# Nine pairs of token tiles instead of six in seven block products, with a new order for every queue

## The chip, the cores and the metric

The kernel runs on one core of one Trainium2 chip. A core has five engines, each with its own queue of instructions: TensorE (PE; weight loads are shown apart as PEld) does matmuls, VectorE (DVE) and ScalarE (ACT) do elementwise work, GpSimd (POOL) does the same more slowly, and SyncE (SP) issues DMAs. Engines wait for one another through semaphores. The metric is the device time of one execution in microseconds (us). Kernels are compared by the median of several executions.

## The reference

Two stages follow one another. The first is an attention with a window of 128 positions and 4 sink positions that every query sees; the second is a feed-forward layer with a swish-like gate over the 3072 tokens:

```python
scores = scale * np.matmul(q, k.transpose(0, 1, 3, 2))       # 4 batches, 8 heads, 768 positions, 64 wide
keep = is_sink | in_window                                   # 4 sinks, or 0 <= query - key < 128
a = softmax(np.where(keep, scores, -1e9))
attn = np.matmul(a, v)
x = attn.transpose(0, 2, 1, 3).reshape(3072, 512)
h = x @ w_in                                                 # 512 x 2048
g = h * (1.0 / (1.0 + np.exp(-beta * h)))
out = g @ w_out                                              # 2048 x 512
```

## The kernel before

The tokens are worked in eight half batches of 384 (T_ = 0 to 7). A half batch goes through these steps, each with one letter in the script:

- L, C: loads of q, k, v into staging buffers, and casts to bf16 (`load` L482, `cast`, whose copies stand at L405 for ACT, L407 for POOL, L410 for DVE). W: the same for the weights (`load_w` L494, `cast_w`).
- T or X: transposes of q and k, by PE for the first three half batches (L606, copied out by ACT or DVE), by DMA from SP after that (L589).
- S: scores of one or more tiles (L727, or L696 in a form by 64-row bands), the exponential on ACT (L739) into E, and the masks: L748 and L757 on DVE, or L754 on POOL.
- A: the products of E with v (L822) and of the sinks (L811, L795), then the division on DVE (L826, L828). R: the transpose of the result into xT, by PE (L847) or by DMA (L841).
- H: one of 16 slices of the first dense product, four matmuls of 384 columns (L864), a tanh on ACT (L870), and on DVE the product that makes g (L872).
- The second dense product. In the plain form, O, one tile of 128 tokens takes 16 matmuls of 512 columns (L884), in four steps of 4, then a copy out and a store (L893). In the pair form, P and Q, two tiles of 128 tokens are multiplied together as a 2 by 2 block product with seven block products instead of eight (`WP`): a block product is 8 matmuls of 256 columns (L965). The weights' sums T1, T2 and T4 stand in the buffers that staged the weights (L914), and T3 overwrites a quarter of the weights w_out16 (`last_w_sum`, L923, letter V), so V comes after the last plain product. For a pair, DVE makes four sums of g in place (L941), ACT or DVE three copies out of PSUM, and DVE five adds (four at L978, one at L1002). The block products of a pair stand in the order 4, 1, 2, 6, 7, 5, 3; a pair ends with its stores (L982).

Before the change the half batches 0 to 3 use the plain form and 4 to 7 the pair form: `FIRST = 4` gives six pairs, each of two tiles of one half batch, or of the third tiles of two neighbouring half batches (`PAIRS_OF`). Even pairs have the letter P, odd ones Q.

The order of work is written out by hand in strings. `SCRIPT` gives the order in which steps are recorded, and with it the numbers of the instructions and the rotation of buffers. `PE_ORDER` gives the order on PE; its letters s to z and digits are filler matmuls on constants (L1140), which compute nothing. `BANKS` gives the PSUM banks. `QUEUES` gives for ACT, DVE, POOL ("gp") and SP the instructions in their order, each as two digits in base 36. Some steps may stand on one of several engines, and the queue in which their number stands decides: a mask on DVE or POOL, a cast on ACT, DVE or POOL, a store on POOL or SP. `Graph.resolve` puts the semaphore waits in.

`Graph.emit` writes the queues. The last store on SP waits first until the earlier stores ("early") have landed; the program ends when the remaining ones ("late") have.

Of the kernel before, what the change touches and what calls it, by code (L numbers as in the profile page):

```python
# [34 lines left out]
class Graph:  # L35
# [241 lines left out]

SCRIPT = ("LLbLWLWLWLWLWLWLWLLWLLCCCCCCCCCBHTHHHTHTTHSHHHHSHHSHHHLWLWLWLLLLLAALWLAAHWOLWORLOLWRWULORROLCCCHHLHC"
          "CCHLHCOLHLCHHLCHHLTOLCTOCTOLCSCTLXXXXOCXOOCXSSCHHCAAHHCALARHLHOLROLORLRHLOOCXSOLCXOCXHCXSCXHCXHHHLHH"
          "LCHHLALRHRRHRHOCLCHHLCXHCXSOOLSLOOHLCXAAOCXHHRARROHCXOCXHOHOCOLOLOHHLLARHHLHHLLCHHLCHLHCXOLOCXSCXOOC"  # L280
          "XOCXOOCXSHLHCHLHHLHHLHHLHHLHHLHCHLHCOCXALCXOCXRRROROCXSCXOCXOOSOOCVAPRALHLHHHHAAHHRRCHPCPHHHHHPRHHHP"
          "PPSQQSHHHHHQQHHARHHHHRHRRHQHQHQHPPPPPPPHHHHHHHHHHQHHHQHHQHQQQQPPPPPPPQQQQQQQ")
# [4 lines left out]
BANKS = ("1740015236014523017646726136523054242315025450170467670132014560173462457371653706153776316745267452"  # L287
         "3002405057403613742674523014567230145023116757654030145231014574302711230656517245062245672303670145"
         "4502176436375401670514501672452375120145207370345213470456456701331016723015264327051670523511676245"
         "45023176523417605304271640135403")  # L290
QUEUES = {"act": ("010w0305070z16101119121b1e1h1i1k1n1w1q1t32303133272a3c3l3p3q2h3v3u3y3a3e3g4c493m3i3s41434547384j4h4f"
                 "4p4m4w4t4y5q4r625h675b696c6h5l6k6p6t6v65716z8c6g6e5z8l8e748n787a7d7h7k8z8w7z818487887x7n8v9a96979tbf"
                 "9i9f9l9ecd9ya9ada4a1akahafamaratb6babdbkbmbrd7bvbyc1c6c9dec5d3etcfcqczcsd5d9dgdidpdrdudwe1e7e3eagjei"
                 "eheoelhhfbfefiflfnecfqfsfvfxf2f8f5g0g2g5g7gagde0gghziuh6h9hchsixhmhphli9i6ibifidilinisizj1hjj3j5j7jb"
                 "jdjfjxk0kllslvjojrjujnk2k8k5kbkdkfkhkjkol1kql3l5l7lalilelmlqm6m8mamemgmcmkmimzmomtmmmqn5mvmxn1n3n7ng"
                 "njnunxnznl"),
          "dve": ("0x0y151813141f1x1d1y1c1z1l1p1m1o201s1r1u232124223525282629393d3k3o3r2b2c3x3b3f3h3z402q4a2s3j3n3t4244"
                 "462x4d3748364g4q4i5658575d595e5f5g5m614s505i684u5j5s6i6a5p6d5t6l5r6u6n6w646q5v728d5w70aq8f7c8o8m6s7j"
                 "7i7o8x907l8283867v7g858h898a8j8i8k5u8q8t8r8u9294989u9r9p9ha79g9n9va0aaaea59ca6a29m9kalaiagbh8bana3as"
                 "aub7bbbebl5xbnawbsayfhaxazb2b3b0b1bxbwc0bzapc2c8c7c3cackcbclcmcvcwcicndmdncocgcrd1ctdad0d6dhdjdqdsdv"  # L300
                 "dxe2e4e8ebf0ekejenemeqfceffffjfmfoftfrfwfyeyevhvg1g3g6g8gbgeghf9gngogtgpgqgrgugsi0i1ivhwh7j9jhjijjh4"
                 "h8iyhdhnhaiai7icigieimioitj0j2j4j6j8jcjejghxhyhoi3jyjzk1jlihiji4kmknlglhlkikiiltlolulwlxjsjplzjtjwly"
                 "m0k4k3k9jvkahukckekgkikkm1ksktkwkukpkvkxkykzkrl4l2l6m2l8m4lblfljm7lrlnm9mbmfmhmdmrmjmsmlmpn0mumnn6mw"
                 "myn2n4n8n9nanbncnhninenknvnwnynmnnnonpnqo0o2o3o4o6nso8"),
          "gp": ("0b0c0g0h0l0t0u0v0i0e0r0m0k0n0s0f0j0d0o0q0p171a1g1j1v342i2k2m2o4b2u4e3w4l4k4o4n666f6m7775796y8g7e7p7m"
                 "609z9jabbjbg7y8p9x9bbpbtced8erepe6faf3f7f6f4dbexglhqhthfgwgigyfghbgchehrjkjmjqiwk6irk7lllpm3m5ndnro5"
                 "nto9"),
          "sp": ("0002040608090a2d2e2f2g2j2l2n2p2r2t2v2w2y2z4v4x4z51525354555a5c5k5n7q6b5o635y766x6j6r6o7bdk807r7t7s7u"
                 "737w918y95938sao9s99aja87f9w9q9dacav9ob8ccbcb9b5biboc4b4cjd4cpbqe9cxbud2cudycydodtdlesdze5ddchegdceu"
                 "f1edewezgkdfg4h0h1h2h3fpgffufzg9fkeefdgmhih5hghkgzgxi2i8ipjaiqgvi5l0lcl9ldnfo1o7")}  # L310


def _program(nc, G, sb, ps, q, k, v, w_in, w_out, beta, out):
# [706 lines left out]
    def xl(hb):  # L1020
        if hb:
            if hb >= CUT:
# [158 lines left out]
```

## Time and profile before

| what | us |
|---|---|
| runs | 217.56, 219.13, 219.31 |
| median | 219.13 |
| the profiled execution | 218.22 |
| its span | 216.5 |
| PE busy in it | 207.1 |
| DVE busy | 166.9 |
| ACT busy | 145.5 |
| POOL busy | 53.8 |

The span runs from the first to the last instruction that the profile shows; the execution's own time is 1.7 us longer. Busy time of PE counts matmuls that are under way; since matmuls overlap one another, a busy PE is not always at its full rate. A group of the profile is a line of the kernel with its engine, operation and tiles; its row gives the count, the busy time, the mean duration in ns, and the engine's idle time just before, with what ended it.

### The profile page before, as it was taken

To read this page: it belongs to the slowest core of one execution; us is meant where nothing else is said; L and a number is where in the kernel's file an instruction comes from. 1 tells how busy PE (TensorE), PEld (TensorE's weight loads), DVE (VectorE), ACT (ScalarE), POOL (GpSimd) and SP (SyncE) were. 2 spreads that over 40 slices of the span, in tenths; PEclk is the share of its full clock that TensorE was granted. 3 is DMA by queue.
4 is the path that set the end of the run, shared out by engine and by line. 5 is a ranking of instruction groups with operands and counts; after the bars stand their busy time and mean duration, and the time that the engine had idled before them with its cause. 6 is when DMAs were issued, how large, how long until landed. Compare 5 with 4: busy or idle time off the path is not lost.

```text
span 216.5 us, 5121 instructions
## 1 busy us (share of the span) xinstructions
PE 207.1 (96%) x2022; PEld 131.2 (61%) x2040; DVE 166.9 (77%) x377; ACT 145.5 (67%) x252; POOL 53.8 (25%) x106
## 2 busy tenths in 40 slices
PE   8979999999999999999999999999999999999991
PEld 3546557555555455546654455865798666668881
DVE  1689899898794379966782587989898998788961
ACT  2899989959973696484585788488626957655210
POOL 7123653012610027100300117014802221000012
PEclk9999999999999999999999999999999999999999
DMA  6999999999989999947896797869985434100223
GB/s 189 257 326 368 353 268 345 380 289 214 215 200 124 221 208 210 188 102 158 151 200 129 148 225 182 173 143 254 193 177 117 98 118 113 40 3 0 97 76 121
DMA packets 94992, 39.90 MB, mean 184 GB/s; under 512 B 82088, under 2 KB 89528, under 8 KB 94968
## 3 DMA queue, kind: packets, MB, share of 16 engines
q1 hardware_dynamic: 92504, 34.33, 71.4%
q0 software_dynamic: 1376, 4.46, 6.4%
q10 hardware_dynamic: 1088, 0.79, 1.2%
q8 instruction: 16, 0.26, 0.5%
q14 instruction: 8, 0.07, 0.1%
HBM read 27.37 MB, written 6.29 MB: 156 GB/s over the span
## 4 chain that ended last, share of the span: by engine, by line
PE 74%; ACT 8%; DVE 8%; DMA 6%; issue 1%; SPq 1%; POOLq 0%; POOL 0%; ACTq 0%
PE P L864 31%; PE P L965 17%; PE P L884 13%; PE P L822 4%; DMA wst<-in_moe_w_out_dram 4%; PE P L696 3%; ACT E L739 3%; PE P L1140 3%; DVE g L872 2%; ACT qkT L405 2%; DMA xT<-onorm 2%; ACT t L870 1%; DVE E L757 1%; DVE E L748 1%; PE P L606 1%
## 5 line engine op out<-in xcount | busy, mean ns | idle before, releaser
L864 PE MATMUL P<-xT,w_in 128*128 128x384 bf16 x512 | 88.4, 326 | 0.9 <-DMA xT<-onorm 0.3
L870 ACT ACTIVATE t<-P,hbeta 128x384 f32<-128x384 f32 x128 | 67.5, 587 | 18.4 <-PE P L864 8.5
L872 DVE SCALAR_TENSOR_TENSOR g<-t,P 128x384 bf16<-128x384 f32 x128 | 64.8, 549 | 13.4 <-ACT t L870 12.6
L864 PEld LDWEIGHTS P<-xT,w_in 128*128 128x128 bf16 x512 | 48.4, 98 | 36.0 <-DMA xT<-onorm 1.4
L739 ACT ACTIVATE E<-P 128x1024 bf16<-128x1024 f32 x44 | 42.9, 1036 | 3.5 <-PE P L696 3.2
L884 PE MATMUL P<-w_out,g 128*128 128x512 bf16 x177 | 43.3, 379 | 1.0 <-issue 0.3
L405 ACT ACTIVATE osb<-P 128x256 f32<-128x256 f32 (+1 forms) x29 | 13.6, 476 | 33.0 <-PE P L965 19.3
L884 PEld LDWEIGHTS P<-w_out,g 128*128 128x128 bf16 x192 | 17.6, 98 | 18.8 <-issue 0.5
L757 DVE TENSOR_TENSOR E<-E,maskT 128x512 bf16<-128x512 bf16 x48 | 19.9, 447 | 8.3 <-ACT E L739 8.2
L754 POOL TENSOR_SCALAR_AFFINE_SELECT E<-E 128x512 bf16<-128x512 bf16 x24 | 16.0, 681 | 35.8 <-ACT E L739 35.8
L965 PE MATMUL P<-w_out,g 128*128 128x256 bf16 x192 | 24.3, 273 | 0.0
L965 PEld LDWEIGHTS P<-w_out,g 128*128 128x128 bf16 x192 | 18.5, 98 | 2.8 <-issue 0.2
L407 POOL TENSOR_SCALAR_AFFINE_SELECT q<-q_stage 128x512 bf16<-128x512 f32 x8 | 5.5, 693 | 56.1 <-DMA q_stage<-in_q_dram 56.1
L965 PE MATMUL P<-wst,g 128*128 128x256 bf16 x144 | 18.4, 273 | 0.0
L941 DVE TENSOR_TENSOR g<-g 128x1024 bf16<-128x1024 bf16 x24 | 16.3, 687 | 1.4 <-PE P L965 1.1
L828 DVE TENSOR_TENSOR onorm<-P,rden 128x384 bf16<-128x384 f32 x32 | 16.7, 546 | 0.3
L822 PEld LDWEIGHTS P<-vaug,E 128*128 128x128 bf16 x352 | 14.0, 97 | 2.8 <-DVE E L748 0.8
L982 POOL DMA_DIRECT2D out_dram<-osb x11 | 6.0, 543 | 37.8 <-DVE osb L978 32.3
L822 PE MATMUL P<-vaug,E 128*128 128x65 bf16 x352 | 15.1, 193 | 0.3 <-DVE E L748 0.3
L965 PEld LDWEIGHTS P<-wst,g 128*128 128x128 bf16 x144 | 13.8, 98 | 2.2
L978 DVE TENSOR_TENSOR osb<-P,osb 128x256 f32<-128x256 f32 x24 | 10.1, 422 | 4.4 <-PE P L965 4.2
L407 POOL TENSOR_SCALAR_AFFINE_SELECT vaug<-v_stage 128x512 bf16<-128x512 f32 x12 | 8.8, 731 | 10.3 <-DMA v_stage<-in_v_dram 10.2
(75 smaller groups left out, 168.1 us busy)
## 6 DMA issues: line engine op xcount, KB each, us to landing
v_stage<-in_v_dram SPq DMA_DIRECT2D x24, 256.0 KB, 5.0
out_dram<-osb POOLq DMA_DIRECT2D x16, 256.0 KB, 3.0
q_stage<-in_q_dram SPq DMA_DIRECT2D x15, 256.0 KB, 4.1
k_stage<-in_k_dram SPq DMA_DIRECT2D x15, 256.0 KB, 4.8
wst<-in_moe_w_in_dram SPq DMA_DIRECT2D x5, 512.0 KB, 8.2
wst<-in_moe_w_out_dram SPq DMA_DIRECT2D x4, 512.0 KB, 8.5
g<-in_moe_w_out_dram SPq DMA_DIRECT2D x4, 512.0 KB, 7.2
q_stage<-in_q_dram SPq DMA_DIRECT2D x2, 768.0 KB, 7.9
```

What stands on the lines that cost most here:

```text
L405: return lambda e: e.activation(dst, src, AF.Copy, bias=0.0, scale=scale)
L739: add("act", lambda e, src=src, dst_=dst_: e.activation(dst_, src, AF.Exp, bias=0.0, scale=SCALE), act_ns(1024), w=[("E", z)] + [("m", z, ...
L754: any_of({"gp": (lambda e, dd=dd, sg=sg: e.affine_select(dd, dd, [[0, n] for n in dd.shape[1:-1]] + [[sg, 128]], ALU.is_ge, 0.0, base=min( ...
L757: "dve": (lambda e, d=d, tri=tri: e.tensor_tensor(d, d, tri, ALU.mult), 340)},
L822: e.matmul(A[:, c0:c0 + D + 1], E[t_ % NE][:, i, hh, :], vaug[vz][:, kb % NK, 2 * hp + hh, :], start=a, stop=o, skip_group_check=True), 31,
L828: add("dve", lambda e: e.tensor_tensor(onorm[on][:, :, :, :].rearrange("p m h d -> p (m h) d"), av[:, :, 0:D], rden[on][:, :].unsqueeze(2) ...
L864: add("pe", lambda e, c=c: e.matmul(hp, w_in16[:, c, m * 128:(m + 1) * 128], xT[:, c, t0:t0 + HALF], start=(c == 0), stop=(c == 3)), mm_ns ...
L870: add("act", lambda e: e.activation(tt[ti][:, :], hp, AF.Tanh, bias=0.0, scale=hbeta[:, m:m + 1]), act_ns(HALF) + 93, r=["hbeta"], w=[("t" ...
L872: add("dve", lambda e: e.scalar_tensor_tensor(gt[T_ % NG][:, m, :], tt[ti][:, :], 1.0, hp, ALU.add, ALU.mult), dve_ns(HALF), r=[("t", ti)] ...
L884: add("pe", lambda e, m=m: e.matmul(P[:, bk, :], gt[T_ % NG][:, m, t * 128:(t + 1) * 128], w_out16[:, m, :], start=(m == 0), stop=(m == NM ...
L941: fn = lambda e: e.tensor_tensor(g_of(n, d), g_of(n, x), g_of(n, y), op)
L965: add("pe", lambda e, i=i: e.matmul(P[:, bk, 0:HN], lhs[:, i, :], rhs[:, i, :], start=p not in (2, 3) and i == 0, stop=i == 7, skip_group_ ...
```

## The change

`FIRST` goes from 4 to 2. Half batches 0 and 1 keep the plain form, 2 to 7 use the pair form, so there are nine pairs. V moves ahead accordingly, to a place behind the second half batch's plain products. `PE_ORDER`, `BANKS` and `QUEUES` are new from beginning to end, and `SCRIPT` from its third line on; they were found by a search in a model of the chip. In `emit`, the late stores are named by their place in the order instead of as the last two. One line is added there, so lines behind it have a number higher by one.

By count of instructions the new order differs in these groups (lines as before the change):

| engine and group | before | after |
|---|---|---|
| PE L884, 512 columns | 192 | 96 |
| PE L965, 256 columns | 336 | 504 |
| PE fillers L1140 | 34 | 33 |
| fillers ahead of the first transposes | 14 | 19 |
| DVE sums L941 | 24 | 36 |
| DVE adds L978 and L1002 | 30 | 45 |
| DVE masks L757 | 48 | 27 |
| POOL masks L754 | 24 | 45 |
| DVE casts of q, k, v, 512 columns | 28 | 18 |
| ACT copies out, 512 and 256 columns | 12 and 17 | 4 and 26 |
| stores on POOL and on SP | 16 and 6 | 6 and 16 |

```diff
     def emit(self, nc, block, sems):
         stores = [o for o in self.ops if o.dma and o.dma.startswith("do")]
         last = [o for o in stores if o.eng == "sp"][-1]
-        late = {o.dma: self.final[o.dma] for o in stores[-2:]}
+        late = {o.dma: self.final[o.dma] for o in stores if o.seq > last.seq}
+        late[last.dma] = self.final[last.dma]
         early = {o.dma: self.final[o.dma] for o in stores if o.dma not in late}
...
-FIRST = 4
+FIRST = 2
...
-PE_ORDER = ("0sssssssssssss.0sss.uu..vv.z.zz.....4w4ww..xx....BvTTT..TzSHHHSHHHHHHHHSHHHHAAAHRARRORHHHHHHOHHOHHHH"
-            "OOOHTTTHOOSTHHOOSOSOAOAOARAOORRROHOHOOOSOOOSHHHHHHHHHHHHHOOHAOOOSOOSOOOAAOAOHAHHHHHHHHHHHHHHHOOOOOSO"
-            "OOHHHHHHHHHOSOHHHHHHHOAOPPSPPPPSHHHHHHHHHHHHHHHHPAAQQAAQQQQPQPSPPPSPHHHHHHAHHHHHHHHPHHHHHHHHHHQQHHHH"
-            "HHQHHQQQPPQQQPPPPQQQQPQ")
+PE_ORDER = ("ssssss0sss0ssssssss..3vvv....uuu.....uu.u.zzz.z.BTT.T..T.SHHHHSHHHHSHHHHHHHHAAARARORRHHHHHHOHHHHOHOH"
+            "HHHHOOTTOOTTOOSOSOSOOOAOAOAAOORRRROHOSOOOSHHHHHHHHHHHHHHHAPPSPPPPSPHHHHHHHHHHHHHHHHAAAAQQPPQQQPPSQPP"
+            "SQHHHHHHHHHHHHHHHHAQQPQQSQQSQHHHHHHHHHHHHHHHHAAAAQQPPQQQQPPQSPPSPHHHHHHAHHHHHHHHHHHHHHHHHHHHHHHHPPHH"
+            "PPPPQQPPQQQPQPPPPQP")
...
```

More of the change, by code (lines that the diff above doesn't have):

```diff
@@ L287 @@
[L287 to L310, printed above, removed]
@@ new lines @@
+          "LCHHLALRHRRHRHOCLCHHLCXHCXSOOLSLOOVHLCXAAPCXHHRARRPHCXPCXHPHCPLPHLPHARHHLLHLHLCHHLCLHHLSLCXQQLCXCXQP"
+          "CXCXQCXQCQQCSLHHLHHLHHLHLHHLHHLHCHLHCXHHCXPALCXCXPCXRRRPRPCXSCPQPCSQQLAQHHRAHHHCAAHHRRHQQHQHHHHRHHHS"
+          "PPPSPPHHHHHPPHHARHHHHRHRRHQHQHQHQQQQHHHHHHHPHPHHPPHHHPHHPHPQQQQQQQPPPPPPP")
+PE_ORDER = ("ssssss0sss0ssssssss..3vvv....uuu.....uu.u.zzz.z.BTT.T..T.SHHHHSHHHHSHHHHHHHHAAARARORRHHHHHHOHHHHOHOH"
+            "HHHHOOTTOOTTOOSOSOSOOOAOAOAAOORRRROHOSOOOSHHHHHHHHHHHHHHHAPPSPPPPSPHHHHHHHHHHHHHHHHAAAAQQPPQQQPPSQPP"
+            "SQHHHHHHHHHHHHHHHHAQQPQQSQQSQHHHHHHHHHHHHHHHHAAAAQQPPQQQQPPQSPPSPHHHHHHAHHHHHHHHHHHHHHHHHHHHHHHHPPHH"
+            "PPPPQQPPQQQPQPPPPQP")
```

27 lines of the change are left out of this document (24 added, 3 removed).

## The prediction

> **What bounds the kernel now.** I read the sums of the page first, then the busy time by 10 us windows, then the chain that ended last in order of time, and only then groups and waits.
>
> ```profile
> span 216.5 us, 5121 instructions
> PE 207.1 (96%) x2022; PEld 131.2 (61%) x2040; DVE 166.9 (77%) x377; ACT 145.5 (67%) x252; POOL 53.8 (25%) x106
> 10.00:20.00 10.00, 8.40 (x123) 5.70 (x127) 9.15 (x26) 9.55 (x18) 2.61 (x5) 1.00 1.10 328
> 20.00:30.00 10.00, 9.53 (x84) 5.11 (x86) 8.45 (x19) 9.36 (x17) 6.34 (x8) 1.00 1.10 336
> 30.00:40.00 10.00, 9.85 (x121) 6.65 (x118) 9.56 (x24) 9.68 (x16) 2.63 (x4) 1.00 0.97 335
> ...
> 150.00:160.00 10.00, 10.00 (x111) 7.76 (x109) 9.07 (x21) 6.14 (x13) 6.17 (x11) 1.00 1.05 195
> ...
> 70.19 2.59 PE P L884 x12
> 102.33 9.11 PE P L864 x56
> 196.33 14.86 PE P L965 x136
> ```
>
> The columns of a window are the busy us of PE, PEld, DVE, ACT and POOL, then granted clock, DMA share and GB/s. Two regimes show. From 10 to 40 us ACT is full (9.55, 9.36, 9.68 of 10): it makes casts, copies and exponentials, and PE waits for it, partly on filler matmuls. From about 40 us PE is full to the end. The chain shows PE at its streaming rate there: 2.59/12 = 0.216 us for a 512-column matmul of L884, 9.11/56 = 0.163 us for a 384-column one of L864, 14.86/136 = 0.109 us for a 256-column one of L965. The granted clock is 1.00 throughout. So behind 40 us only less PE work helps; ahead of it only less ACT work, or ACT work that waits less.
>
> **PE work.** Three more pairs of token tiles go from plain second products to the seven-product form. The orders of the two kernels count L884 from 192 to 96 matmuls and L965 from 336 to 504; all other real matmuls stay. 96 x 0.216 = 20.7 us go, 168 x 0.109 = 18.4 us come: **-2.4 us**, 0.8 a pair. Fillers are 34 before and 33 after, one 256-column matmul less, 0.1 us, which I leave out.
>
> **The other engines.** What a pair costs elsewhere:
>
> ```profile
> L757 DVE TENSOR_TENSOR E<-E,maskT 128x512 bf16<-128x512 bf16 x48 | 19.9, 447 | 8.3 <-ACT E L739 8.2
> L941 DVE TENSOR_TENSOR g<-g 128x1024 bf16<-128x1024 bf16 x24 | 16.3, 687 | 1.4 <-PE P L965 1.1
> L754 POOL TENSOR_SCALAR_AFFINE_SELECT E<-E 128x512 bf16<-128x512 bf16 x24 | 16.0, 681 | 35.8 <-ACT E L739 35.8
> L978 DVE TENSOR_TENSOR osb<-P,osb 128x256 f32<-128x256 f32 x24 | 10.1, 422 | 4.4 <-PE P L965 4.2
> L405 ACT ACTIVATE osb<-P 128x512 f32<-128x512 f32 x12 | 7.3, 606 | 11.1 <-PE P L884 11.0
> L405 ACT ACTIVATE osb<-P 128x256 f32<-128x256 f32 x17 | 6.4, 385 | 22.0 <-PE P L965 19.3 <-DMA out_dram<-osb 2.6
> L410 DVE CAST vaug<-v_stage 128x512 bf16<-128x512 f32 x10 | 5.1, 521 | 0.5 <-DMA v_stage<-in_v_dram 0.5
> ```
>
> DVE gets 12 sums of L941 (12 x 0.687 = 8.2), 12 adds of L978 and 3 of L1002 (15 x 0.422 = 6.3): 14.6 us. It gives up 21 masks of L757 (9.4) and 10 casts of q, k, v at about 0.5 (5.0). So DVE stays at some 167 us; the room for the sums is bought by moving 21 masks to POOL, at 0.681 instead of 0.447 us each. POOL gets 14.3 us of masks and hands 10 of its 16 stores to SP: well under the span either way. ACT changes 8 big evacuations for 9 small ones (-4.8 + 3.5), takes 5 casts of v, 2 of q and 3 copies of qkT, and loses a k cast, a w_out cast and an xT copy: about +2.4 us. None of them becomes the bound by its sum. Moved masks and sums I therefore cost at nothing, hidden by PE's matmuls; the price if that cover fails is in the rivals.
>
> **The head.** Here the orders cost something.
>
> ```profile
> 0.85 5.20 PE L1140 MATMUL P<-const-bfloat16-1.0 128*128 128x256 bf16 x14 [0.85 <-PEq L1163]
> 5.89 0.33 PE L606 MATMUL P<-ident,q 128*128 128x128 bf16 x3
> ...
> 6.22 0.93 PE L1140 MATMUL P<-const-bfloat16-1.0 128*128 128x256 bf16 x4
> 6.99 0.33 PE L606 MATMUL P<-ident,q 128*128 128x128 bf16 x3
> 4.47 0.41 DVE L410 CAST k<-k_stage 128x384 bf16<-128x384 f32 x1
> 8.74 1.02 ACT L739 ACTIVATE E<-P 128x1024 bf16<-128x1024 f32 x1
> 9.66 1.25 ACT L405 ACTIVATE qkT<-P 128x384 bf16<-128x384 bf16 x3
> 26.48 1.12 DVE L410 CAST w_in<-g 128x1024 bf16<-128x1024 f32 x1
> 28.16 1.99 ACT L870 ACTIVATE t<-P,hbeta 128x384 f32<-128x384 f32 x4 [0.64 <-DVE g L872]
> 37.55 0.49 ACT L405 ACTIVATE xT<-P 128x384 bf16<-128x384 bf16 x1 [0.24 <-PE P L847]
> ```
>
> Fillers held the first transposes already: the casts were done at 4.88 (4.47 + 0.41), the transposes ran at 5.89. Now 19 fillers instead of 14 stand ahead of them, 4 of 512 columns and one of 256 more. The four at 6.22 took 6.99 - 6.22 = 0.77 us for 3.5 of 512 columns, 0.22 each; 4.5 x 0.22 = 1.0 us. So the first transposes run at about 6.9, and the second ones, which now follow without fillers, at about 7.25 (6.99 before). ACT then has three copies of 0.38 (1.25 us for three overlapped ones) and two casts of 0.41 ahead of its first exponential: 7.3 + 3 x 0.38 + 2 x 0.41 gives 9.3, and with two hand-overs of about 0.15 each **9.6 instead of 8.74**, 0.85 us late.
>
> From the first exponential to the last copy of xT for the second half batch (37.55), ACT's list gets 2 copies of qkT and one tanh more and one copy of xT less: 2 x 0.39 + 0.46 - 0.39 = **0.85 us**. Together ACT is 1.7 us later at this point if it waits as before. It need not: it lost 0.64 us at 28.16, behind DVE products that stood behind a 1.12 us cast of w_in, and 0.24 at 37.55. Both casts of that kind go to POOL in the new order. I take those 0.9 us as gained, which leaves 0.8 us; the ends are 0 (all cover found) and 1.7.
>
> Behind this point PE has 2.2 us less to do (2.4 less 0.2 for the slightly different place in its order). **-2.2 + 0.8 = -1.4 us.**
>
> **Transposes by DMA.** SP issues them one after another, with loads and stores between:
>
> ```profile
> 114.01 1.26 SPq L841
> 115.31 0.58 SPq L482
> 115.94 4.68 DMA xT<-onorm
> 120.66 0.34 PE P L864
> PEld P L864 <- DMA xT<-onorm: 1.4, 3, 0.7
> ```
>
> A transpose holds the queue for 1.26 us, a load for 0.58. SP gets the 10 stores that POOL had; 10 x 0.58 = 5.8 us of its time. PE waited 0.7 us at most for xT, at 120. I counted, in matmuls at the rates above, what PE does in each order between the last value product and the first use of its xT: there 14 us instead of 18 to 21; at the other four groups 8, 9, 14 and 7 us, instead of 12, 8, 12 and 8. I take no change; the ends are -0.7 (this wait goes) and +1.4 (two of five groups late by as much).
>
> **The end.** Both orders end on two third products of two pairs, two adds, one store from POOL and one from SP that waits for the earlier stores. The wait list in `emit` is written differently and holds two stores again. No change.
>
> **DVE beside POOL.** The trace has a price for masks on POOL that no sum shows:
>
> ```profile
> 9.98 0.42 DVE L757 TENSOR_TENSOR E<-E,maskT 128x512 bf16<-128x512 bf16 x1
> 21.61 0.71 DVE L757 TENSOR_TENSOR E<-E,maskT 128x512 bf16<-128x512 bf16 x1 [0.51 <-ACT E L739]
> 20.98 1.06 POOL L407 TENSOR_SCALAR_AFFINE_SELECT w_in<-wst 128x1024 bf16<-128x1024 f32 x1 [0.91 <-DMA wst<-in_moe_w_in_dram]
> PEld P L864 <- DVE g L872: 1.0, 3, 0.5
> L941 DVE TENSOR_TENSOR g<-g x24: 677/688/693, 138.1 to 207.7; 128x1024 bf16<-128x1024 bf16 x24
> ```
>
> The same mask takes 0.42 us alone and 0.71 when it starts while POOL works (POOL until 22.04): 0.3 us lost. The sums of L941, in the row with min/median/max, never met it: 677 to 693 ns for all 24. A lone block is worth 0.3 us; the ends are 0 (DVE has slack) and, for the 21 moved masks, 21 x 0.3 = 6.3 us. I take 0, since PE waited for DVE's products 1.0 us in all, and carry the upper end into a rival. The Trainium skill, page "SBUF — State Buffer", section "Who interferes with whom", says that a DVE instruction with two SBUF inputs and a POOL instruction that reads SBUF exclude each other, the later one blocking fully. The 0.71 us mask agrees with it; by it alone, with every moved mask meeting a sum, the sum would be -1.4 + 6.3, a slower kernel.
>
> **The sum.** The profiled execution took 218.22 us (span 216.5). 218.22 - 1.4 = **216.8 us**. The median of the three runs shown is 219.13, 0.9 above it; against that 216.8 is 1.1% less. 1%, some 2.2 us, is about what a measurement of this kernel can tell from no change, since its runs spread from 217.56 to 219.31.
>
> **Rivals.** (1) *The full saving*: ACT's delay is covered, 2.4 us go, and the 0.7 us wait at 120 too: 218.2 - 3.1 = 215.1. For it: PE is full behind 40 us. Against it: ACT's list is longer where ACT is the bound. (2) *The head eats it*: ACT is 1.7 us late and one more xT comes 0.5 us late: 218.2 - 2.2 + 1.7 + 0.5 = 218.2. For it: 9.36 and 9.68 us of ACT in 10. Against it: waits of 0.64 and 0.24 us that a better order avoids. (3) *Slower*: between products and sums of one pair PE waits for DVE, as the sums meet POOL's masks. Place: the second-product groups between 85 and 165 us, where masks and sums now lie together. Price: 0.3 us a block, decisive from 1.4/0.3 = 5 blocks on PE's path, over 1% slower (221.3) from 15. With 17 of them, 218.2 - 1.4 + 5.1 = 221.9. For it: 36 sums instead of 24, 45 POOL masks instead of 24, DVE at 9.07 and POOL at 6.17 of 10 in a window such as 150 to 160. Against it: none of 24 sums met a mask before, with POOL at 6.17 of 10 in that window.
>
> **Chances.** Forecast 0.40, full saving 0.17, eaten by the head 0.20, slower 0.23. The forecast's own spread is 0.8 us to each side (216.0 to 217.6), so 0.24 of its 0.40 fall under 216.9. Faster by over 1%: 0.24 + 0.17 = 0.41. Slower by over 1% (over 221.3): 0.21 of the last rival and 0.02 of the second, 0.23. Within 1%: 0.36. The range from 214.9 to 221.8 leaves out the low half of the first rival and half of the last, some 0.19.
>
> **What the profile after would show.** L884 x96 and L965 x504 at the same durations; the first exponential near 9.6 us; ACT still full from 10 to 40 us, without a 0.64 us stop behind w_in; the last xT copy of the second half batch about 0.8 us later than 37.55; PE at 10.00 in the windows behind 40. L941's mean above 0.69 us, and PE waiting for L941 or L978, would speak for the slower rival; xT among PE's waits with more than 1.4 us for SP's queue. I am wrong if PE's waits between 40 us and the end grow by more than 1.5 us, or if the head's delay is not carried by ACT.

## The result

The changed kernel is slower. It was compared with the kernel before three times: first by itself, then in the second and in the fifth group of the experiments below, which ran on two different chips. The ratio of times was 1.0154 (95% interval 1.0117 to 1.0191; medians 221.18 against 218.66 us), 1.0133 (1.0078 to 1.0189; 221.49 against 218.04) and 1.0049 (1.0016 to 1.0082; 219.75 against 218.42). The ratio on record is not the quotient of the two medians; that is 1.0115, 1.0158 and 1.0061. So it loses between 0.5 and 1.5%, 1.1 to 3.4 us, and one comparison is good to 0.3 to 0.6%. The forecast was 216.8, a gain of 1.4 us. The profiled execution took 220.31 us with a span of 218.6.

The changed kernel's page, first the span and the sums of the engines, then the groups that answer to those of before (busy us and mean ns behind the bar, then the idle time before them):

```profile
span 218.6 us, 5316 instructions
PE 206.0 (94%) x2102; PEld 139.1 (64%) x2111; DVE 171.2 (78%) x373; ACT 147.5 (67%) x260; POOL 65.5 (30%) x122
...
L966 PE MATMUL P<-w_out,g 128*128 128x256 bf16 x288 | 36.1, 273 | 0.3 <-DVE osb L979 0.3
L966 PE MATMUL P<-wst,g 128*128 128x256 bf16 x216 | 27.9, 273 | 0.0
L942 DVE TENSOR_TENSOR g<-g 128x1024 bf16<-128x1024 bf16 x36 | 24.8, 699 | 1.9 <-PE P L966 1.4
L885 PE MATMUL P<-w_out,g 128*128 128x512 bf16 x89 | 22.2, 379 | 0.5 <-issue 0.2
```

PE was 96% busy before and is 94% busy now: 504 small matmuls (288 and 216) and 96 large ones (7 of them missing from the records) are there as planned, and PE stands idle more. Where it stands idle is in the windows behind 130 us. First the kernel before, then the changed one (us of the window, then PE, PEld, DVE, ACT, POOL, clock, DMA share, GB/s):

```profile
130.00:150.00 20.00, 19.89 (x225) 13.44 (x226) 16.86 (x39) 14.79 (x27) 5.99 (x10) 1.00 0.84 182
150.00:170.00 20.00, 20.00 (x254) 16.02 (x252) 17.91 (x41) 11.32 (x21) 7.83 (x13) 1.00 0.84 172
170.00:190.00 20.00, 20.00 (x181) 13.15 (x179) 17.12 (x41) 13.88 (x26) 4.15 (x7) 1.00 0.28 80
```

```profile
130.00:150.00 20.00, 18.19 (x224) 13.25 (x223) 15.63 (x36) 12.69 (x23) 4.74 (x9) 1.00 0.77 146
150.00:170.00 20.00, 19.96 (x251) 15.95 (x250) 17.98 (x41) 11.22 (x21) 5.82 (x10) 1.00 0.87 186
170.00:190.00 20.00, 17.95 (x161) 11.02 (x159) 15.70 (x38) 14.20 (x28) 1.87 (x3) 1.00 0.33 93
```

PE was idle there for 0.11 us before (20.00 - 19.89) and is for 3.90 now (1.81 + 0.04 + 2.05). The groups of PE's waits and the chain that ended last say what it waits for. The changed kernel's waits of PE between 130 and 190 us (total, times, longest), and its chain from 160 us on (start, duration, what):

```profile
PE P L865 <- DMA xT<-onorm: 2.0, 2, 1.6
PE P L697 <- DMA qkT<-q: 1.0, 1, 1.0
PE P L865 <- ACT vaug L406: 0.8, 1, 0.8
```

```profile
168.95 3.68 DMA xT<-onorm
...
172.68 3.59 PE P L865 x21
...
181.70 3.76 DMA xT<-onorm
...
185.51 4.56 PE P L865 x27
```

For the kernel before, the same question (PE's waits, 130 to 190 us) has no answer row at all, and its chain there is PE alone. In the changed kernel the last transposes of xT for the seventh and the eighth half batch, issued by SP, end the wait.

To put numbers on it I use PE's **lost time**: the moment at which the n-th w_in matmul runs, less the PE work that the order puts ahead of it, at the durations of the prediction (0.163, 0.216 and 0.109 us for the dense products, and medians of the trace for the small ones; all PE work is 203.0 us before and 200.4 after). The **late loss** is its growth from the 320th w_in matmul (the end of the fifth half batch) to the 512th (the end of the eighth).

| kernel (profiled execution) | lost at the first H | first H of the second half batch | at the 320th | at the 512th | late loss |
|---|---|---|---|---|---|
| before | 5.65 | 6.79 | 8.54 | 8.87 | 0.33 |
| changed | 6.92 | 7.97 | 8.70 | 13.39 | 4.69 |
| changed, second group | 6.59 | 7.86 | 9.89 | 14.00 | 4.11 |
| changed, fifth group | 6.92 | 8.73 | 9.35 | 12.54 | 3.19 |

The saving of PE work is there (203.0 - 200.4 = 2.6 us), but 3 to 4.7 us are lost behind the fifth half batch, where the kernel before lost 0.3.

### The profile page after: what moved, and what is told of

It reads as the page before. It is cut to its first block, busy times and chain, and to the rows that moved or that the text cites. A ratio compares the mean times of both kernels' runs of the same rounds, so it can differ in the third digit from the quotient of the medians.

```text
span 218.6 us, 5316 instructions
## 1 busy us (share of the span) xinstructions
PE 206.0 (94%) x2102; PEld 139.1 (64%) x2111; DVE 171.2 (78%) x373; ACT 147.5 (67%) x260; POOL 65.5 (30%) x122
## 4 chain that ended last, share of the span: by engine, by line
PE 73%; DMA 8%; ACT 6%; DVE 6%; SPq 4%; issue 1%; POOLq 0%; POOL 0%; DVEq 0%
PE P L865 32%; PE P L966 22%; PE P L885 9%; SPq L483 4%; PE P L823 4%; DMA xT<-onorm 3%; DMA k_stage<-in_k_dram 3%; PE P L697 2%; ACT t L871 2%; ACT E L740 2%; DMA v_stage<-in_v_dram 2%; DVE osb L979 1%; ACT w_out L406 1%; DVE g L873 1%; PE P L607 1%
## 5 line engine op out<-in xcount | busy, mean ns | idle before, releaser
L755 POOL TENSOR_SCALAR_AFFINE_SELECT E<-E 128x512 bf16<-128x512 bf16 x45 | 30.0, 689 | 43.8 <-ACT E L740 43.8
L966 PE MATMUL P<-w_out,g 128*128 128x256 bf16 x288 | 36.1, 273 | 0.3 <-DVE osb L979 0.3
L966 PEld LDWEIGHTS P<-w_out,g 128*128 128x128 bf16 x288 | 27.6, 98 | 4.3 <-DVE osb L979 0.5
L966 PE MATMUL P<-wst,g 128*128 128x256 bf16 x216 | 27.9, 273 | 0.0
L942 DVE TENSOR_TENSOR g<-g 128x1024 bf16<-128x1024 bf16 x36 | 24.8, 699 | 1.9 <-PE P L966 1.4
L885 PE MATMUL P<-w_out,g 128*128 128x512 bf16 x89 | 22.2, 379 | 0.5 <-issue 0.2
L966 PEld LDWEIGHTS P<-wst,g 128*128 128x128 bf16 x216 | 20.7, 98 | 2.8 <-ACT E L740 0.2
L979 DVE TENSOR_TENSOR osb<-P,osb 128x256 f32<-128x256 f32 x36 | 15.1, 421 | 7.6 <-PE P L966 7.0
L983 POOL DMA_DIRECT2D out_dram<-osb x6 | 3.3, 551 | 36.7 <-DVE osb L979 36.4
L758 DVE TENSOR_TENSOR E<-E,maskT 128x512 bf16<-128x512 bf16 x27 | 11.8, 464 | 3.1 <-ACT E L740 3.1
L408 POOL TENSOR_SCALAR_AFFINE_SELECT vaug<-v_stage 128x512 bf16<-128x512 f32 x10 | 6.8, 684 | 17.9 <-DMA v_stage<-in_v_dram 17.9
```

The costliest lines, as they stand in the source:

```text
L408: return lambda e: e.affine_select(dst, src, [[0, n] for n in src.shape[1:]], ALU.is_ge, 0.0, base=0, channel_multiplier=0)
L755: any_of({"gp": (lambda e, dd=dd, sg=sg: e.affine_select(dd, dd, [[0, n] for n in dd.shape[1:-1]] + [[sg, 128]], ALU.is_ge, 0.0, base=min( ...
L885: add("pe", lambda e, m=m: e.matmul(P[:, bk, :], gt[T_ % NG][:, m, t * 128:(t + 1) * 128], w_out16[:, m, :], start=(m == 0), stop=(m == NM ...
L942: fn = lambda e: e.tensor_tensor(g_of(n, d), g_of(n, x), g_of(n, y), op)
L966: add("pe", lambda e, i=i: e.matmul(P[:, bk, 0:HN], lhs[:, i, :], rhs[:, i, :], start=p not in (2, 3) and i == 0, stop=i == 7, skip_group_ ...
L979: add("dve", lambda e: e.tensor_tensor(d, src, u, ALU.add), 335, r=[r], w=[w], x=[("B", bk)], after=base[w])
```

## The theory and its rivals

SP's queue in the stretch that decides the seventh half batch, from the timeline (start, duration); first before, then after:

```profile
141.76 0.59 SPq L482 DMA_DIRECT2D q_stage<-in_q_dram  x1
...
146.54 4.05 SPq L482 DMA_DIRECT2D v_stage<-in_v_dram  x3
150.63 1.84 SPq L589 DMA_TRANSPOSE qkT<-q  x1
...
160.53 1.28 SPq L841 DMA_TRANSPOSE xT<-onorm  x1
```

```profile
140.26 0.58 SPq L483 DMA_DIRECT2D v_stage<-in_v_dram  x1
140.88 2.55 SPq L842 DMA_TRANSPOSE xT<-onorm  x2
143.48 0.58 SPq L483 DMA_DIRECT2D v_stage<-in_v_dram  x1
...
152.15 1.55 SPq L983 DMA_DIRECT2D out_dram<-osb  x2
153.75 1.49 SPq L590 DMA_TRANSPOSE qkT<-k  x1
...
162.95 0.58 SPq L983 DMA_DIRECT2D out_dram<-osb  x1
163.57 1.19 SPq L483 DMA_DIRECT2D v_stage<-in_v_dram  x2
164.80 5.42 SPq L842 DMA_TRANSPOSE xT<-onorm  x4
```

SP hardly pauses in either: between 134 and 168 us it has one pause of 0.8 us before and none after. The transposes of q and k begin at 153.75 instead of 150.63, the four of xT at 164.80 instead of 160.53, 4.3 us later, while PE comes to the first H product of this half batch at about the same time, 169.86 before and 170.40 after. Of the 4.3 us, 1.7 are there when the sixth half batch's xT has been issued (at 143.44 instead of 141.71); in between, the new order has three more stores (2.1 us of issue) and two more loads (0.9 us), and its transposes hold SP a little less. **Theory G**: loads, transposes and stores are one supply through SP's in-order queue and the DMA engines; it is as full as before, the new order brings it later, and the saved PE time is waited away. A larger amount of bytes does not explain it: between 90 and 170 us there are 26 loads, 34 transposes and 9 stores before, 13.4 MB, and 27, 33 and 8 after, 13.3 MB.

The rivals: the ten stores that moved to SP (theory C by their place in the queue, D by their bytes); the one store that POOL issued at 133.37 us among the q transposes (A); instruction fetches that fall on transposes (E); one v load among the xT transposes; the head; the order of work on other engines (K).

## The experiments

The kernels of one group ran on one chip beside the kernel before. Since the changed kernel's own ratio differs between groups, kernels are compared within a group unless said otherwise; late losses are read from profiled executions, one for each kernel. In the diffs of queues, the two-digit numbers are instructions.

**One undoing at a time.** First group, four kernels. POOL's store early:

```diff
 "gp":  ... g4 g1
+           ft
            eh f9 ...
        ... f7 fi
-           ft
            iv ic ...
```

> The changed kernel with one store moved on POOL: the store of osb that POOL issued at 133.37 us, while SP issued the last two q transposes (133.24 and 134.55, landed 138.64 and 139.04), goes seven places ahead, to about 126 us, where SP issues loads. Theory A (a store issued on POOL holds the transposes that SP has under way): the two q transposes land by about 137, the stall of 1.15 us ahead of the band products at 137.88 goes, and the time falls by 0.8 to 1.2 us against the changed kernel, to about 220.1 on its median of 221.2. Theory B (these transposes are late only because SP issues them late, behind loads and stores of its own queue): the stall stays, time within 0.3 us of 221.2.

Seven stores from SP to POOL:

```diff
-"sp": do, dt, fv, k1, jx, in, ii at their places
+"gp": ... cb do bp dt ct ... g1 fv ii eh ... ic in jx k1 i5 ...
```

> The changed kernel with the seven stores of paired tiles that SP issued from 99.84 to 162.95 us taken off SP and given to POOL at places where POOL stands idle (about 100, 101, 126 twice, 147 three times). On SP they held 2.07 + 0.75 + 0.58 + 1.08 + 0.43 + 0.58 + 0.58 = 6.1 us of issue. Theory C (the place on SP is what costs): the xT transposes of the seventh half batch are issued 2 to 3 us earlier, its stall of 1.8 us at 170.72 goes, time 2 to 3.5 us below the changed kernel, 217.7 to 219.2. Theory D (the bytes of the stores cost, whatever queue issues them, since all share the DMA engines): within 0.8 us of 221.2.

The same stores on SP, but narrow; in seven of the output tiles columns 64 to 511 are not written:

```diff
-                store(tb, ob, slice(0, NOUT), [bl, bh])
+                store(tb, ob, slice(0, 64 if n in (0, 2, 3) else NOUT), [bl, bh])
...
-                store(ta, oa, slice(0, NOUT), [al, ah])
+                store(ta, oa, slice(0, 64 if n < 4 else NOUT), [al, ah])
```

> The changed kernel with the same seven stores left on SP in their places, with all their waits, but each writing only the first 64 of 512 columns (the rest of those seven output tiles is not written). Theory C (the place on SP costs): seven issues and their waits are still there, time within 0.7 us of 221.2. Theory D (bytes): 7 x 224 KB less between 100 and 165 us, transposes and loads behind them land up to 0.5 us each earlier, time 1.5 to 3 us below, 218.2 to 219.7. If neither this nor the run with the stores on POOL moves the time by 0.7 us, the moved stores are not the cause.

Five fillers less at the head:

```diff
-PE_ORDER = ("ssssss0sss0ssssssss..3vvv...
+PE_ORDER = ("ssssss0sss0sss..3vvv...
```

> The changed kernel with five of the filler products at its head left out (14 ahead of the first transposes instead of 19, as in the kernel before). My prediction's step on the head says that the five cost 0.85 us for good: time 0.8 to 1.2 us below the changed kernel, 220.0 to 220.4. Rival: the head is taken up by later waits, since at 130 us the changed kernel was only 0.2 us of lost time behind although it had been 1.2 behind at 38 us: time within 0.4 us of 221.2. A second rival: the fillers keep the granted clock up, and without them the head is slower, up to 0.5 us above.

| kernel | ratio to before | late loss |
|---|---|---|
| POOL's store early | 1.0055 (1.0022 to 1.0087) | 3.98 |
| seven stores on POOL | 1.0033 (0.9997 to 1.0070) | 3.30 (fifth group) |
| seven stores narrow | 1.0027 (0.9999 to 1.0056) | 2.47 |
| five fillers less | 1.0071 (1.0044 to 1.0098) | 2.62 |

The profiled execution of the seven stores on POOL in this group took 221.38 us, the longest of eleven, with a late loss of 4.64; the table has the one of the fifth group.

Against 1.0154 all four look like gains of 0.8 to 1.3%. That all four give as much is suspicious, and the level they were held against was taken elsewhere: the fifth group, below, has the changed kernel itself at 1.0049. Among themselves the four differ by 0.4%, less than the width of an interval. Theory A isn't shown either: with POOL's store early PE's stall ahead of the band products at 139 us is 0.52 us where the first profile had 1.15, but the unedited kernel of the second group has 0.52 there too. The head's run did show where the head's time goes. ACT's timeline, first the changed kernel, then with five fillers less:

```profile
7.18 0.52 ACT L406 ACTIVATE q<-q_stage 128x384 bf16<-128x384 f32 x1 [2.08 <-DMA q_stage<-in_q_dram]
7.94 1.25 ACT L406 ACTIVATE qkT<-P 128x384 bf16<-128x384 bf16 x3 [0.23 <-PE P L607]
...
9.89 1.03 ACT L740 ACTIVATE E<-P 128x1024 bf16<-128x1024 f32 x1
```

```profile
7.33 0.52 ACT L406 ACTIVATE q<-q_stage 128x384 bf16<-128x384 f32 x1 [2.44 <-DMA q_stage<-in_q_dram]
7.76 1.23 ACT L406 ACTIVATE qkT<-P 128x384 bf16<-128x384 bf16 x3
...
9.70 1.03 ACT L740 ACTIVATE E<-P 128x1024 bf16<-128x1024 f32 x1
```

The first exponential comes at 9.89, and without the five fillers at 9.70: taking them out gives 0.2 us, not 0.85. ACT's new list has a cast of q ahead of its first copies, and that cast waits until past 7 us for its load; without the fillers it is this cast that holds the copies.

**Fetches and the v load.** Second group: the changed kernel again, and three edits. Fetches of instructions show in the DMA queues of the page (queue, kind: packets, MB, share); the changed kernel has

```profile
q8 instruction: 16, 0.26, 0.6%
q14 instruction: 8, 0.07, 0.1%
```

and the kernel before as many of both. A packet of q8 has 16 KB, and the trace has one for each 250 PE instructions or so (16 packets, 4246 matmuls, weight loads and waits on PE).

> The changed kernel as it is, beside the kernel before and the next three kernels on one chip, as the level for them. Both theories: a ratio of 1.012 to 1.019 to the kernel before, if the first comparison holds on another chip; the two transposes of xT that land last in the seventh and the eighth half batch late by 0.7 us or more where an instruction fetch falls on them.

The fillers cut into pieces:

```diff
+    def filler(e, n, b):
+        k = n if n == 2 else 3 if b == 0 else 4
+        at = [128 * n * j // k for j in range(k + 1)]
+        for x, y in zip(at, at[1:]):
+            ins = e.matmul(P[:, b, x:y], one.to_broadcast([128, 128]), one.to_broadcast([128, y - x]),
+                           start=True, stop=True)
+        return ins
```

> The changed kernel with the filler products at its head cut into pieces, three in place of one ahead of the first transposes and four behind them: the same columns, some 150 more PE instructions, so that PE reaches each of its instruction fetches (16 of 16 KB, one for each 256 PE instructions or so) about 150 instructions, some 7 us, earlier in its work. In the changed kernel fetches began at 134.64, 170.14 and 183.07 and transposes under way then landed after 5.41 and 4.49 (q), 3.68 and 3.76 us (xT), where one that meets nothing lands after 2.36. Theory E (the fetch holds the transposes, and so a large part of the loss): fetches at about 128, 163 and 176, the last xT transposes of the seventh and eighth half batch land after 2.4 us, the stalls of 1.80 and 0.58 us shrink by 1.2 and 0.5, time 1 to 2.5 us below the changed kernel. Rival F (the fetch is a bystander, the order on SP alone decides): the same landings, time within 0.5 us of the changed kernel. A dearer head would show ahead of the first H product (21.95 in the changed kernel) and is taken off.

The v load behind the xT transposes, its cast on ACT later:

```diff
-"sp":  ... hz i0 g6 hy i2 f6 ...      "act": ... iq h1 it ... js jy ...
+"sp":  ... hz i0 hy i2 g6 f6 ...      "act": ... iq it ... js h1 jy ...
```

> The changed kernel with the one load of v that SP issues among the xT transposes of the sixth half batch (140.26 us) put behind them, and its cast on ACT seven operations later, so that ACT does not wait for it. If that load is what makes the first H product of this half batch late (xT transposes landed 140.00, 141.31, 144.13, 144.55, the gap of 2.8 us holding the load): they land 1.3 spaced, the last by about 143.3, the stall of 0.99 us at 143.17 goes, time 0.5 to 1 us below the changed kernel. If what is saved there is waited for again at the xT of the next half batch, which SP issues back to back behind it: within 0.4 us of the changed kernel.

Four edits together (POOL's store early, the v load, five fillers less, the other fillers in four pieces):

> Four edits together: POOL's store early, v load behind the xT transposes, five filler products less at the head, the others cut into four pieces so that the fetches come earlier. If the loss of 4.5 us is these transposes' delays one by one, the gains add: 3 to 4.5 us below the changed kernel, which is level with the kernel before or up to 1 us below it. If one chain through SP's queue holds all of them, the gains don't add: 1 to 2 us below the changed kernel.

| kernel | ratio to before | lost at the 320th | late loss |
|---|---|---|---|
| changed kernel | 1.0133 (1.0078 to 1.0189) | 9.89 | 4.11 |
| fetches earlier | 1.0110 (1.0066 to 1.0154) | 11.24 | 2.34 |
| v load behind xT | 1.0114 (1.0069 to 1.0159) | 9.36 | 3.86 |
| four together | 1.0192 (1.0137 to 1.0248) | 10.85 | 2.90 |

The fetch is no bystander. The DMA queues while the last two xT transposes of the eighth half batch are under way, in the changed kernel from 181.5 to 186 us (first profile), then with the fetches earlier from 182.3 to 186 (queue: packets, MB, share of 16 engines; the last row has the median us to landing):

```profile
q8 instruction: 1, 0.02, 1.4%
q14 instruction: 1, 0.01, 1.0%
...
xT<-onorm SPq DMA_TRANSPOSE x2, 3.1
```

```profile
q14 instruction: 1, 0.01, 0.7%
...
xT<-onorm SPq DMA_TRANSPOSE x2, 2.4
```

With a fetch of PE's (q8, begun at 183.07) the last transpose took 3.76 us to land, without it 2.4; in the shifted kernel this fetch began at 177.52, the transposes of 181.2 and 182.5 landed after 2.36 and 2.41, and the chain there goes through without a wait at the eighth half batch:

```profile
177.34 1.56 PE P L823 x48
178.89 11.21 PE P L865 x69
```

The late loss falls by 1.8 us, as theory E had it, but the pieces of filler, each with its weight load, cost 1.4 us by the 320th product, so the time stayed. And a shifted fetch is a fetch elsewhere: in the four-together run one fell at 167.53 among the xT transposes of the seventh half batch (landings of 4.77, 3.52 and 3.39 us), and PE stood 2.0 us there. That run, with the four edits together, was the slowest of the group, so the expectation that the gains add fell, and so did the gain of 1 to 2 us that one chain would have left. The v load did what its first half says and no more: the stall ahead of the sixth half batch's first H product went, PE still waited for xT twice (2.0 us in all), and the time is within 0.2% of the changed kernel's.

**The fetch by waits, and the loads cut.** Third group. Waits that add PE instructions without matmuls:

```diff
+                if eng == "pe":
+                    for lo, hi in ((251, 283), (359, 435), (359, 391), (719, 779)):
+                        if lo <= n < hi:
+                            handle.wait_ge(sems["act"], 1)
+                            handle.wait_ge(sems["dve"], 1)
```

> The changed kernel with two waits on counts long since reached set before 200 PE instructions, most of them w_in products between 25 and 70 us, so that PE's program is about 200 instructions longer there and every later fetch of PE instructions comes 8 us earlier in the work; head and all queue orders are untouched. The earlier run with cut fillers did the same but paid 1.6 us at the head up to the fifth half batch. Theory E (a fetch that falls on the last transposes of a group makes half of the late loss): fetches near 162 and 175 in place of 170.1 to 175.0 and 183.07 to 184.06; the last xT of the eighth half batch lands after 2.4 us, its stall (0.58, 1.06) goes; from the fifth half batch's first H product to the last H product 73.6 us, as with the cut fillers, where the changed kernel took 75.6; time 1.3 to 2.2 us below the changed kernel, if the waits themselves are free beside products of 163 ns. Rival: the waits cost, 200 x 51 ns on PE's sequencer = 10 us, and as much of it as isn't hidden is added.

The same with the store, the v load and the head:

> The same waits, and with them five filler products less at the head, POOL's store early and the v load behind the xT transposes. If the delays are separate: 1.5 us for the fetches, 0.8 for the head, 0.5 to 1 for the two others, 3 to 3.5 us below the changed kernel, 217.5 to 218.5, level with the kernel before. If the supply through SP's queue is one chain that swallows them: 1 to 2 us below the changed kernel, 219.5 to 220.5.

Both took 1.0207 of the kernel before (1.0160 to 1.0254, 1.0162 to 1.0253): the rival held, and the store, the v load and the head gave nothing on top. Between the first H product of the second half batch and that of the third, lost time grew by 2.4 us (8.51 to 10.95), where the changed kernel has 0.4 in the fifth group (8.73 to 9.12), 0.5 in the first profile and 1.3 in the second group: 1.2 to 2 us for the 108 wait instructions set there. The 60 waits among the third half batch's products cost nothing (0.44 against 0.45). The eighth half batch's last xT landed after 2.4 us here too, but a fetch at 141.79 met the xT of the sixth and the v load among them (landings of 3.95 and 4.38 us), and PE stood 1.6 us there, by the profile for the cast of this v. So a shift of the fetches moved the loss about, and in none of these runs did it gain time that could be told.

The loads of the last three half batches cut to two of eight heads:

```diff
             dst, keys, ns = stg[n][z][:, i, :, :], [("stb", n, z, i)], NV0 if hb < 2 else 1092
+            if hb >= 5:
+                src, dst = src[:, 0:2, :], dst[:, 0:2, :]
```

> The changed kernel with the loads of q, k and v for the last three half batches (27 loads of 256 KB, from about 95 us on) cut to two of eight heads: the same number of issues in the same places, a quarter of the bytes; the other heads of these half batches are computed from stale stage tiles. Theory G (loads and transposes are supplied by SP and the DMA engines no faster than before, and so the PE time saved is waited away at the xT transposes from 138 us on): the stalls at 138, 143, 171 and 185 us (4.5 us together) shrink to under 1.5, time 3 to 4.5 us below the changed kernel, 216.8 to 218.3. Rival K (the stalls come from the order of other engines' work, or from issue time on SP that does not depend on bytes): at most 1 us below.

> The kernel before with the same cut of the same loads. Its large stalls lie before 121 us, and of its lost PE time behind 130 us only 1 to 1.5 us stand at first products that wait for xT: time 0.5 to 1.5 us below the kernel before. Theory G then has the changed kernel with cut loads 0.5 to 2.4 us below this one (the PE work that it saves), where uncut it is 3 us above. Rival K: both gain alike, and the changed kernel stays 2.5 to 3 us above.

| kernel | ratio to before | lost at the 320th | late loss |
|---|---|---|---|
| changed, loads cut | 0.9938 (0.9904 to 0.9972) | 10.04 | 1.64 |
| before, loads cut | 0.9971 (0.9935 to 1.0007) | 7.94 | 0.70 |

This one decides between G and K. The changed kernel with cheap loads took 217.46 us (median), and its ratio lies 1.1 to 2.2% below the three of the uncut one; the kernel before gains 0.3% from the same cut, no more than its interval. The uncut changed kernel did not run in this group, but the fourth group, below, repeats the comparison on one chip. With cheap loads the changed kernel is no longer the slower one (217.46 against 217.97, with intervals that overlap). Windows of the changed kernel with cut loads:

```profile
130.00:150.00 20.00, 20.00 (x236) 14.43 (x234) 17.02 (x40) 14.45 (x27) 7.02 (x13) 1.00 0.52 123
150.00:170.00 20.00, 19.96 (x252) 16.06 (x251) 18.17 (x42) 11.11 (x21) 2.92 (x5) 1.00 0.38 91
170.00:190.00 20.00, 18.95 (x167) 11.65 (x165) 16.57 (x38) 15.15 (x28) 1.87 (x3) 1.00 0.24 73
```

The DMA share falls from 0.77 and 0.87 to 0.52 and 0.38, and PE's idle time in the first two windows from 1.85 to 0.04 us, with the same orders on every engine. The xT transposes of the seventh half batch start at 161.38 instead of 164.80:

```profile
161.38 5.08 SPq L844 DMA_TRANSPOSE xT<-onorm  x4
```

Between 90 and 170 us a load of q, k or v holds SP for 0.88 us on average in the changed kernel, and for 0.58 with a quarter of the bytes; in the same stretch the transposes of q land after 3.4 and after 2.5 us (medians). So both parts of the supply got faster, SP's issue and the DMA engines, and this run does not separate them. What is left, 1.05 us in the last window, is the wait at the eighth half batch: there a fetch at 180.70 met the last transpose, which landed after 4.40 us. Rival K, the order of other engines' work or an issue time on SP that does not depend on bytes, would have kept the stalls.

**Do the undoings add?** Fourth group, with the fillers, POOL's store and the seven stores undone together, with the v load as well, without the seven stores, and the fillers with the loads cut:

> Three undoings of the change together, each of which alone gave something: five filler products less at the head (1.0071 of the kernel before), POOL's store early (1.0055) and the seven stores on POOL in place of SP (1.0033); the changed kernel itself stood at 1.0154 and 1.0133. Theory G with three separate burdens on one supply: 0.996 to 1.000 of the kernel before. If each of them only frees the same wait: 1.003, as the best of them.

> The three and, as a fourth, the v load of the sixth half batch behind its xT transposes with its cast later on ACT (alone 1.0114, no gain that could be told). Theory G: the order of transposes and loads within a full queue gives nothing, within 0.003 of the run without it. Rival: with the stores gone the stall ahead of the sixth half batch's first H product is a term of its own, 0.5 to 1 us below that run.

> Only the five filler products less and POOL's store early, the seven stores left on SP. Theory G: 1.001 to 1.005 of the kernel before (0.8 % and 0.8 % off 1.0143, less what both free); the difference to the run with the seven stores on POOL is what those stores cost on SP, 0.003 to 0.008. Rival (the two free the same wait): 1.006.

> The changed kernel with the last three half batches' loads cut to a quarter (0.9938 of the kernel before) and five filler products less at the head. With the supply cheap, nothing later takes the head up: if my head step (0.85 us for good) holds where PE is the bound, 0.85 to 1.3 us below that run, 0.988 to 0.990. If the head is taken up by other waits all the same: 0.993 to 0.995.

| kernel | ratio to before | late loss |
|---|---|---|
| head, store, seven stores | 1.0038 (1.0003 to 1.0072) | 3.54 |
| the same and the v load | 1.0074 (1.0038 to 1.0111) | 4.10 |
| head and store | 1.0067 (1.0038 to 1.0096) | 4.27 |
| loads cut, five fillers less | 0.9942 (0.9914 to 0.9969) | 1.56 |

Nothing adds, and the late loss stays at 3.5 to 4.3. The loads cut show the same as in the third group, now beside kernels with full loads on the same chip: 0.9942 against 1.0038 to 1.0074, with a late loss of 1.56. With cheap loads the five fillers give nothing either (0.9942, and 0.9938 with them in the third group).

**The level, or the stores?** Fifth group, the changed kernel and the seven stores on POOL, on one chip:

> The changed kernel as it is, on one chip with the next kernel: so far it was compared with the kernel before on two other chips (1.0154 and 1.0133) than those on which the undoings ran. If those levels hold on every chip: 1.012 to 1.017. If chips differ and the undoings were measured on a kinder one: 1.005 to 1.010.

> The changed kernel with the seven stores on POOL in place of SP, again, beside the changed kernel on the same chip. Theory G with the stores as a burden of their own on SP: 0.007 to 0.012 below the ratio of the changed kernel in this comparison. If their gain was the chip's: within 0.004 of it.

1.0049 (1.0016 to 1.0082) and 1.0032 (1.0004 to 1.0060): nearly all of the stores' gain had been the level. SP's timeline in the changed kernel here, and with the stores gone from SP:

```profile
149.46 1.00 SPq L483 DMA_DIRECT2D k_stage<-in_k_dram  x1
...
164.84 5.50 SPq L842 DMA_TRANSPOSE xT<-onorm  x4
```

```profile
152.38 2.55 SPq L483 DMA_DIRECT2D k_stage<-in_k_dram  x1
...
165.78 5.38 SPq L842 DMA_TRANSPOSE xT<-onorm  x4
```

Without the stores the transposes of xT start at 165.78. This execution took 221.39 us, the longest of thirteen, and was late long before: by 1.0 us at its first H product and by 2.5 at the sixth half batch's first xT (139.74 instead of 137.27). From that xT to the seventh's it needs 26.0 us where the changed kernel has 27.6, so the stores gone from SP bring 1.5 us here, of the 2 to 3 expected; in the first group's execution of the same kernel (136.66 to 164.30, 27.6 us) they bring nothing. The issue of a load that took 1.00 us now takes 2.55 (2.61 there), while POOL's stores are under way. The time is what lets theory C fall: 0.2% less than the changed kernel, within the intervals, with a late loss of 3.30 instead of 3.19. D is not shown either: the narrow stores' 1.0027 can't be told from the 1.0033 and 1.0055 beside it.

What stays open: which item of the new SP order costs how much. Cheaper loads free the late loss; taking single items out of the order or moving them did not. No kernel tried, at full bytes, was faster than the kernel before.

## Why the prediction was wrong

- **PE work, -2.4.** Right: 203.0 to 200.4 us by the orders, 0.2 more than said.
- **The other engines at nothing.** Right as to the cost. DVE's sum was 4 us off (171.2 busy, where I had some 167) and POOL has 65.5, but PE's waits behind 130 us name neither, apart from a cast on ACT that itself waited for a load.
- **DVE beside POOL.** Taken as nothing, and it was; the slower rival fell as a mechanism, though its sign came out. Of the 36 sums one met POOL:

```profile
L942 DVE TENSOR_TENSOR g<-g x36: 679/691/1119, 89.4 to 209.6; 128x1024 bf16<-128x1024 bf16 x36
```

The one of 1119 ns (from 122.34 us on) was held by a mask on POOL (122.09 to 122.91), as the rule of the Trainium skill, page "SBUF — State Buffer", section "Who interferes with whom", has it; PE ran without a stop beside it (its chain from 121.53 us on is w_in matmuls alone), so it was not on PE's path.

- **The head, +0.8.** About right in size, incomplete in its cause. The first exponential came at 9.89 (9.6 said, 8.74 before), the second half batch's first H product ran 0.97 us later (38.32 against 37.35), and lost time at the 320th product is 0.2, 0.8 and 1.4 us above before in the three profiles. But I held the fillers alone to blame for the late copies; without five of them the first exponential comes only 0.2 us earlier, since a cast on ACT, which I left out, waits for its load nearly as long.
- **Transposes by DMA: "I take no change; the ends are -0.7 ... and +1.4".** This is the step that failed. The late loss rose by 2.9 to 4.4 us. Two things were wrong in it. I priced the moved stores as issue time on SP, 5.8 us, and asked whether PE had work to cover it; I did not follow when SP could *reach* the xT transposes, behind loads of q, k and v whose issue takes longer the more bytes are under way (0.88 us a load on average between 90 and 170 us, 0.58 with a quarter of the bytes, and 2.44 for one at 146.60). In the changed kernel the sixth half batch's xT transposes end at 143.44 instead of 141.71, then come the loads, then q and k, and the seventh's xT start 4.3 us later. And the end of the range was taken from the one wait that before showed (0.7 us), although SP's queue paused for only 0.8 us between 134 and 168 us, so that a delay there is handed on whole and that wait is no bound for it. The second rival ("one more xT 0.5 late") had the place but not the size. Cut loads, which leave every instruction in its place, left 1.64 us of late loss where the three uncut profiles have 3.2 to 4.7, which shows that most of it is the supply. PE's idle time from 40 to 210 us grew from 1.56 to 4.64 us, past the 1.5 that the prediction named as the sign of being wrong.
- **The sum.** In the changed kernel's profile of the fifth group, with the smallest loss: -2.6 of work, +0.8 up to the 320th product, +2.9 behind it, +0.2 behind the last H product: +1.3. The first profile has -2.6 + 0.2 + 4.4 + 0.2 = +2.2, and its span grew by 2.1. That the range still held the time (221.18 in the first comparison) is luck: the slower rival, whose mechanism did not happen, stretched it upward.

## What to carry over

When an engine is full and its work is cut, look at what supplies it before counting the gain: a queue with hardly any idle time beside the full engine (here SP, whose transposes stand behind loads) can set the pace next, and its price is read from when it can reach the critical transfer, not from the sum of its issues. Shrinking the bytes of the suspected supply, with every instruction left in place, tells whether it is the bound, if the kernel before gets the same cut. And hold edits against the changed kernel on the same chip: four undoings looked like gains of 1% because its level had been taken elsewhere.

## What the hardware showed unexpectedly

- A fetch of instructions during the run holds DMA transposes. Transposes of xT that meet nothing land after 2.3 to 2.4 us; with a fetch beginning while they are under way the last of a group landed after 3.68 and 3.76 us in the changed kernel, after 4.24 in the second group and 4.40 with cut loads. The fetches' place follows PE's instruction count: some 150 more PE instructions ahead brought the one near the eighth half batch from 184.06 to 177.52.
- Loads in pieces of 256 bytes move more slowly than stores in pieces of 2 KB. GB/s in 40 slices of the changed kernel, from 147 to 156 us (loads; stores and transposes from 153 us on) and from 174 to 177 us (four stores):

```profile
GB/s 179 192 239 233 237 232 236 234 212 167 107 52 67 117 179 279 280 211 126 129 113 253 288 281 274 286 277 208 187 220 223 234 245 245 302 331 387 419 346 353
```

```profile
GB/s 410 383 410 383 410 410 382 382 437 382 410 410 328 410 382 355 328 437 437 382 328 437 382 382 382 355 410 328 273 246 137 55 0 0 0 0 0 0 0 0
```

The median of the first nine slices is 233 in the first row and 410 in the second. The Trainium skill, page "DMA: Bandwidth & Descriptors", section "Specifications", puts the least transfer at line rate at 512 bytes, and the two rows agree. The direction is not what makes them slow: the weights' loads, mostly in pieces of 1 and 2 KB, moved 378 GB/s from 18 to 24 us. Whether q, k and v in larger pieces would relieve the supply was not tried.

- The same two kernels differ by 0.5% in one comparison and by 1.5% in another, with intervals that do not touch. The first has four runs of each kernel, and its quotient of medians is 1.0115. Whether the chip makes the difference was not tried.
- Redundant waits on PE cost 1.2 to 2 us for 108 wait instructions among the second half batch's products and nothing for 60 among the third's. Why the two differ is open.
